# Opening stage of an attention and two-layer-pair kernel: idle and row-sum products left out, lists written anew, a small load behind each weight half

## The chip, the cores and the metric

The kernel runs on one core of a Trainium2 chip. The metric is the device time of one execution in microseconds (us), measured three times; lower is better. The profile shows five engines that run side by side and wait for each other by semaphores: PE (TensorE: matrix products and, as PEld, the loads of their stationary operand), DVE (VectorE), ACT (ScalarE), POOL (GpSimd, here the issuer of loads) and SP (SyncE, the issuer of most loads and stores).

## The reference

```python
# attention: q, k, v (4, 8, 768, 64), 8 memory keys and values a head
for c in range(nc):                       # chunks of 32 queries
    l_start = max(0, c_start - 16); r_end = min(S, c_end + 8)
    k_full = concat([mem_k, k[l_start:r_end]]); v_full = ...
    scores = scale * q_c @ k_full.T
    scores = scores - max(scores); a = exp(scores)
    a = a / (sum(a) + 1e-9)
    out[chunk] = a @ v_full
x = out as (3072, 512)
h = relu(x @ w_in); x = (s * h * h + b) @ w_out               # 512 -> 2048 -> 512
g = x @ w_gate; out = (g * sigmoid(g) * (x @ w_val)) @ w_out2   # 512 -> 1536 -> 512
```

All data are 32-bit floats. The big products are made of three reduced-precision products each (high times high, high times low, low times high), so every weight and every operand is split into two parts first.

## The kernel before

The tokens are cut into 24 groups of 128 queries (g) and eight blocks of 384 tokens (t). Groups 0 to 5 are the opening stage: their keys and queries come in with a few large loads, are turned on PE against the identity and copied out (`stage_batch_keys`, `stage_batch_queries`; steps K and Q). Then, for each group, follow the scores S (32 products of 32x64, `stage_scores`), the row maximum on DVE, the exponential on ACT, the turning A of the probabilities on PE, the products V with the values (`stage_values`), the division by the row sums on DVE (`stage_normalise`), and the turning X of the result (`stage_turn`), which ACT or DVE round to a high part `xhi`, while DVE makes the residue `xlo` (`stage_x`). Every S, and every V, takes both banks of the pool `ps_a`, so an S or V starts only when the one before it was read out by DVE or ACT.

The first pair of layers has 16 weight slots m (W0 to W15), each loaded in two halves of 512 KB (`load_slot`, `load_w1`) and split by a chain of operations, mostly on DVE (`split`: magnitude, two steps of `t_first`, sign, rest, a rounding copy, a residue). U is the up product of one block with one slot (`first_up`, bank `hp`, 12 products), D the down product (`first_down`, banks `acc`). The first U of block 0 needs X0 to X2, the first of block 1 needs X3 to X5.

For groups 0 to 5 the row sums come from PE: `stage_values` multiplies the turned probabilities with a column of ones as well (line 636), and `stage_sums_out` (lines 658 and 660) reads those sums from the bank. Where a group's name stands in `MOVED` as e0, e6 and so on, ACT makes the sums along with the exponential instead (`stage_exp_heads`). `run_idle` runs products of the identity with itself whose result nobody reads.

A planner (`Plan`) simulates all tasks with fixed durations and emits each engine's instructions in the order it finds. `START` is the order of the opening steps on PE, written out by hand; `LOADS` the order of the big loads on SP; `MOVED` says which tasks go to the second engine of two. SP issues in order and a waiting load holds up those behind it. Values come by POOL's own loads, into three buffers in turn.

Of the kernel before, what the change touches and what calls it, by code (L numbers as in the profile page):

```python
# [30 lines left out]
    "K0 Q0 S0 W24 S1 A0 Q1 V0 A1 S2 X0 K1 V1 A2 X1 V2 S5 X2 S3 U S4 U A3 V3 A4 D X3 V4 D X4 A5 U "  # L31
    "V5 U X5 D U D "
# [12 lines left out]
    "BK1 BK0 C BM BQ01 BQ00 W1 W0 K6_0 BQ10 BQ11 W6 W3 W5 W2 W4 W11 W10 W7 W9 W8 W12 W13 W14 W15 "  # L45
# [15 lines left out]
)  # L61


class Plan:
# [12 lines left out]
    def add(self, engine, length, emit, deps=(), get=(), put=(), lag=0.0, take=(), give=()):  # L77
        t = SimpleNamespace(
            n=len(self.tasks), engine=engine, length=length, emit=emit, get=tuple(get), put=list(put),
# [20 lines left out]

    def run(self):
# [12 lines left out]
        started = []  # L114
        while events:
# [15 lines left out]
            for engine, waiting in ready.items():  # L131
                for item in sorted(waiting) if free[engine] else ():
                    t = self.tasks[item[1]]
                    if all(self.room[r] >= t.get.count(r) for r in t.get):
                        for r in t.get:
                            self.room[r] -= 1
                        waiting.remove(item)
                        free[engine] = False
                        t.start = now
                        started.append(t)  # L140
                        heapq.heappush(events, (now + t.length, 0, t.n))
                        break
# [5 lines left out]
def attention_and_two_mlps(  # L148
# [70 lines left out]
    kept = const.tile([P, PAD + P + PAD + 3], F32, name="ident")  # L219
    padded, sb, ones = (kept[:, a:z] for a, z in ((0, 2 * PAD + P), (2 * PAD + P, 2 * PAD + P + 2), (2 * PAD + P + 2, 2 * PAD + P + 3)))  # L220
    ident = padded[:, PAD:PAD + P]
    make_identity(nc, ident)
    nc.vector.memset(ones, 1.0)
# [19 lines left out]
    def load_slot(sources, name, rows="(k p) f -> p k f"):  # L243

        raw = wp.tile([P, 2, 2 * 512], U32, tag="w", name=f"raw_{name}")
        for n, src in enumerate(sources):
# [6 lines left out]
            else:  # L253
                nc.sync.dma_start(out=raw[:, n], in_=src)
        return raw

    raw1 = {}
    w1 = {}

    def load_w1(m):  # L260
        cols = slice(m * P, (m + 1) * P)
        raw1[m] = load_slot((w_in[:, cols], w_out[cols, :]), f"first{m}", "(p k) f -> p k f")
# [231 lines left out]
    def load_memory_values():  # L494
        for e in range(2):
            nc.gpsimd.dma_start(
                out=lent("keys1")[0:NMEM, 3, e * NP * D:(e + 1) * NP * D].rearrange("p (j d) -> p j d", d=D),
# [3 lines left out]
    def load_values(g, queue):  # L501
# [3 lines left out]
        for e in range(2):  # L505
            p0 = e * KC
            if g < VBUFS(0):
                mem = lent("keys1")[0:NMEM, 3, e * NP * D:(e + 1) * NP * D]
# [59 lines left out]
    def stage_max(g, e):  # L568
        gi = g % GB
        ps = staged[g]["s"][e]  # L570
        if e == 0:
            staged[g]["mx"] = ap_.tile([P, 2, NC, 1], F32, tag="mx", name=f"mx{g}")
# [32 lines left out]
    def stage_exp_heads(g, e):  # L605
        if e == 0:
            staged[g]["rc"] = ap_.tile([P, NC, 2, 1], F32, tag="rc", name=f"rc{g}")
# [18 lines left out]
    def stage_values(g, both=None):  # L626
        at = staged[g].pop("at")
        tv = loaded.pop(g)["v"]
        n = D + (g < EARLY)
        banks = [t[:, -NC * n:].rearrange("p (c s) -> p c s", c=NC) for t in both or two_banks(f"psV{g}")]  # L630
# [13 lines left out]
    def stage_sums(g, done=False):  # L644
        if not done:
            staged[g]["rc"] = ap_.tile([P, NC, 2, 1], F32, tag="rc", name=f"rc{g}")
# [8 lines left out]
    def stage_sums_out(g):  # L655
        staged[g]["rc"] = rc = ap_.tile([P, NC, 2, 1], F32, tag="rc", name=f"rc{g}")
        for e in range(2):
            nc.vector.tensor_scalar(rc[:, :, e], staged[g]["o"][e][:, :, D:], 1e-9, None, op0=ALU.add)
        flat = rc.rearrange("p c e o -> p (c e o)")
        nc.vector.reciprocal(flat, flat)  # L660

    def stage_normalise(g, e):
        if e == 0:
            staged[g]["on"] = ap_.tile([P, 4 * 2 * D], F32, tag="on", name=f"on{g}")
        on, o, n = staged[g]["on"], staged[g]["o"][e][:, :, :D], D // KD
# [895 lines left out]
```

## Time and profile before

| | us |
|---|---|
| three runs | 1212.52, 1213.50, 1213.93; median 1213.5 |
| profiled execution | 1214.94 |
| its span in the trace | 1213.1 |
| PE busy / DVE busy | 1185.6 / 744.9 |

The profiled execution is 1.84 us longer than its span, and 1.4 us longer than the median. PE is busy for 98% of the span, so time can only be lost where PE waits, runs products that aren't needed, or runs at the lower clock. The rows show where: nearly all of it lies before 90 us.

### The profile page before, as it was taken

How to read it: one execution, taken by the hardware profiler on the slowest of the kernel's cores; microseconds unless marked ns; L12 is line 12 of the kernel's file. 1: busy time of each engine (PE TensorE's matmuls, PEld its weight loads, DVE VectorE, ACT ScalarE, POOL GpSimd, SP SyncE). 2: the span in 40 equal slices, each digit the busy share in tenths (PEclk: the TensorE clock that was granted, in tenths of full speed). 3: DMA queues.
4: the chain of work that ended last, by engine and by line, in shares of the span. 5: the costliest groups of instructions: out<-in, count | busy, mean ns of one | idle time of the engine just before them, and what ended most of it. 6: DMA issues, size and time to landing. Idle time of an engine off the chain costs nothing.

```text
span 1213.1 us, 24661 instructions
## 1 busy us (share of the span) xinstructions
PE 1185.6 (98%) x9872; PEld 1130.9 (93%) x9872; DVE 744.9 (61%) x1309; ACT 505.1 (42%) x894; POOL 145.9 (12%) x235
## 2 busy tenths in 40 slices
PE   7699999999999999999999999999999999999998
PEld 6589999999999999999999999999999999999997
DVE  5699976655554445444487956569854367743343
ACT  4336543243333443342276545446433235432332
POOL 4750013222222223120000000000000000000000
PEclk9799999999999999999999999999999999999999
DMA  9754334322222222220356256386555386465351
GB/s 281 177 154 145 113 104 98 68 44 65 42 52 66 44 65 51 44 54 1 113 199 236 121 218 229 122 309 255 201 221 217 127 330 247 153 245 208 108 206 52
DMA packets 160991, 175.49 MB, mean 145 GB/s; under 512 B 101276, under 2 KB 130252, under 8 KB 159852
## 3 DMA queue, kind: packets, MB, share of 16 engines
q1 hardware_dynamic: 153580, 162.54, 40.9%
q0 software_dynamic: 7296, 11.37, 3.8%
q8 instruction: 78, 1.28, 0.4%
q14 instruction: 37, 0.30, 0.1%
HBM read 124.85 MB, written 48.76 MB: 143 GB/s over the span
## 4 chain that ended last, share of the span: by engine, by line
PE 91%; DVE 4%; issue 2%; SPq 1%; DMA 1%; ACT 1%; DVEq 0%; ACTq 0%
PE hp L701 7%; PE acc L701 6%; PE acc L702 6%; PE hp L703 6%; PE hp L702 6%; PE acc L703 6%; PE chain_A L702 6%; PE chain_A L703 6%; PE oacc L703 6%; PE oacc L702 6%; PE chain_A L701 5%; PE oacc L701 5%; PE chain_B L701 4%; PE chain_B L703 4%; PE chain_B L702 4%
## 5 line engine op out<-in xcount | busy, mean ns | idle before, releaser
L701 PE MATMUL hp<-xhi,w_first 128*128 128x384 f32 x512 | 174.5, 341 | 0.0
L701 PE MATMUL acc<-ghi,w_first 128*128 128x384 f32 x512 | 173.1, 338 | 0.4 <-DVE ghi L754 0.4
L702 PE MATMUL acc<-glo,w_first 128*128 128x384 f32 x512 | 171.6, 335 | 0.8 <-DVE glo L763 0.4
L702 PE MATMUL hp<-xlo,w_first 128*128 128x384 f32 x512 | 172.0, 336 | 0.0
L703 PE MATMUL hp<-xhi,w_first 128*128 128x384 f32 x512 | 172.0, 336 | 0.0
L703 PE MATMUL acc<-ghi,w_first 128*128 128x384 f32 x512 | 171.3, 334 | 0.0
L516 POOL DMA_DIRECT2D v<-in_v_dram x190 | 121.9, 649 | 297.3 <-PE psB L634 273.0
L871 ACT ACTIVATE kept<-chain_A 128x384 f32<-128x384 f32 x144 | 70.8, 492 | 184.9 <-PE chain_A L703 184.4
L702 PE MATMUL chain_A<-ops,hi_up 128*128 128x384 f32 x384 | 130.1, 339 | 0.0
L703 PE MATMUL chain_A<-ops,lo_up 128*128 128x384 f32 x384 | 129.4, 337 | 0.0
L701 PE MATMUL chain_A<-ops,hi_up 128*128 128x384 f32 x384 | 128.4, 334 | 0.0
L741 DVE SCALAR_TENSOR_TENSOR r<-r,ident 128x384 f32<-128x384 f32 x89 | 54.5, 612 | 114.0 <-ACT r L730 112.4
L730 ACT ACTIVATE r<-hp 128x384 f32<-128x384 f32 x100 | 49.1, 491 | 170.0 <-PE hp L703 158.1
L703 PE MATMUL oacc<-w_down,glo 128*128 128x512 f32 x288 | 114.6, 398 | 0.0
L702 PE MATMUL oacc<-w_down,ghi 128*128 128x512 f32 x288 | 113.9, 396 | 0.0
L701 PE MATMUL oacc<-w_down,ghi 128*128 128x512 f32 x288 | 112.1, 389 | 0.0
L702 PEld LDWEIGHTS acc<-glo,w_first 128*128 128x128 f32 x512 | 96.1, 188 | 2.0 <-DVE glo L763 1.2
L701 PEld LDWEIGHTS hp<-xhi,w_first 128*128 128x128 f32 x512 | 96.7, 189 | 1.4 <-issue 0.2
L701 PEld LDWEIGHTS acc<-ghi,w_first 128*128 128x128 f32 x512 | 96.1, 188 | 1.6 <-DVE ghi L754 0.7
L876 DVE TENSOR_TENSOR kept<-chain_B,kept 128x384 f32<-128x384 f32 x48 | 26.7, 557 | 114.7 <-PE chain_B L703 112.5
L702 PEld LDWEIGHTS hp<-xlo,w_first 128*128 128x128 f32 x512 | 96.7, 189 | 0.2 <-DVE xlo L696 0.2
L703 PEld LDWEIGHTS hp<-xhi,w_first 128*128 128x128 f32 x512 | 96.7, 189 | 0.0
(171 smaller groups left out, 2270.5 us busy)
## 6 DMA issues: line engine op xcount, KB each, us to landing
ops<-ops_dram SPq DMA_DIRECT2D x56, 768.0 KB
ops_dram<-ops SPq DMA_DIRECT2D x28, 768.0 KB
sum_dram<-o SPq DMA_DIRECT2D x48, 256.0 KB
v<-in_v_dram POOLq DMA_DIRECT2D x162, 56.0 KB, 2.9
raw_first<-in_moe_w_in_dram SPq DMA_DIRECT2D x16, 512.0 KB
raw_first<-in_moe_w_out_dram SPq DMA_DIRECT2D x16, 512.0 KB
o<-sum_dram SPq DMA_DIRECT2D x8, 1024.0 KB
y_dram<-y SPq DMA_DIRECT2D x32, 192.0 KB
```

The source lines that it names most:

```text
L516: queue.dma_start(out=tv[p0 + row:p0 + row + rows, c].rearrange("p (j d) -> p j d", d=D), in_=v[b, e:H:2, first:first + rows, :].rearrange ...
L701: nc.tensor.matmul(o, whi, xhi, start=first, stop=False, skip_group_check=onto)
L702: nc.tensor.matmul(o, whi, xlo, start=False, stop=False, skip_group_check=onto)
L703: nc.tensor.matmul(o, wlo, xhi, start=False, stop=last, skip_group_check=onto)
L730: nc.scalar.activation(out=r, in_=hp, func=AF.Relu)
L741: nc.vector.scalar_tensor_tensor(out=r, in0=r, scalar=s_sb, in1=r, op0=ALU.mult, op1=ALU.mult)
L871: nc.scalar.activation(out=t, in_=st2[n]["A"], func=AF.Copy)
L876: nc.vector.tensor_tensor(out=t, in0=st2[n]["B"], in1=kept, op=ALU.add)
```

## The change

- The 24 idle products (step W24) and the products with ones are left out, and with them the ones column. The row sums of groups 0 to 2 now come from ACT with the exponential (e0, e1, e2), those of groups 3 to 5 from a reduction on DVE over the exponentials (`stage_sums`, new line 664).
- `START`, `LOADS` and `MOVED` are written anew. Q1 now stands ahead of A0, S1 and S2 ahead of K1, V0 behind K1, S4 and V3 ahead of the first U. The constants `s`, `b` and the memory keys are loaded behind the first block of keys, ahead of the second; all queries ahead of all weights. More copies go to DVE: three of the first four key banks, two of A, two of `xhi`.
- `load_slot` with `follow` issues behind each half of a W slot a load of one element into one of two cells. Two loads into the same cell wait for each other, so this small load is issued only once the small load two halves back has landed.
- The planner counts PE's instructions (`words`) and holds PE at every 256th until the next 256 have come (`PAGE`, `FETCH`, `end`). Slots, sums and buffers (`rc0` to `rc2`, `vb0` to `vb2`, `s0` to `s3`) are given back by name. The memory values lie in the `values` buffer. This acts on the order alone.

```diff
 START = (
-    "K0 Q0 S0 W24 S1 A0 Q1 V0 A1 S2 X0 K1 V1 A2 X1 V2 S5 X2 S3 U S4 U A3 V3 A4 D X3 V4 D X4 A5 U "
-    "V5 U X5 D U D "
+    "K0 Q0 S0 Q1 A0 S1 S2 K1 V0 A1 S3 X0 V1 A2 X1 V2 A3 S4 X2 V3 U A4 S5 X3 U V4 A5 D X4 U D V5 "
+    "U X5 D U D "
 )
 LOADS = (
-    "BK1 BK0 C BM BQ01 BQ00 W1 W0 K6_0 BQ10 BQ11 W6 W3 W5 W2 W4 W11 W10 W7 W9 W8 W12 W13 W14 W15 "
+    "BK0 C BM BK1 BQ01 BQ00 K6_0 BQ11 BQ10 W1 W0 W2 W3 W7 W4 W5 W12 W6 W8 W10 W9 W14 W11 W13 W15 "
 )
 MOVED = (
-    "a10 a12 a9 e0 e6 g0_0 ...
+    "a0 a10 a12 a4 a7 a9 e0 e1 e2 e6 e8 g0_12 ...
...
+DEPTH = 2
+PAGE, FETCH = 256, ((45.0, 8.3), (110.0, 4.0), (1e9, 2.5))
...
+    probe = const.tile([1, DEPTH], F32, name="probe")
+    probes = [probe[:, n:n + 1] for n in range(DEPTH)]
...
-    def load_slot(sources, name, rows="(k p) f -> p k f"):
+    def load_slot(sources, name, rows="(k p) f -> p k f", follow=False):
...
                 nc.sync.dma_start(out=raw[:, n], in_=src)
+            if follow:
+                probes.append(probes.pop(0))
+                nc.sync.dma_start(out=probes[-1], in_=s_row)
...
-    def run_idle(n):
-        ps = bank(ps_acc, "acc0", "idle")[:, 0:P]
-        for _ in range(n):
-            nc.tensor.matmul(ps, ident, ident, start=True, stop=True)
...
-                nc.tensor.matmul(banks[e][rows_to, col, :D], at[r, col, rows_to], tv[r, c, j], start=True, stop=True)
-                if n > D:
-                    nc.tensor.matmul(banks[e][rows_to, col, D:], at[r, col, rows_to], ones[r], start=True, stop=True)
+                nc.tensor.matmul(banks[e][rows_to, col], at[r, col, rows_to], tv[r, c, j], start=True, stop=True)
```

PE, the first V. Before, it comes behind Q1, each product with one by ones behind it (psQ are banks of turned queries, psK of turned keys, psV of V):

```order
L343 MATMUL psQ_2_476<-ident,queries_277 64x128 x6
L343 MATMUL psQ_3_484<-ident,queries_277 64x128 x6
L634 MATMUL psV_0_495<-v_150,at_461 32x64
L636 MATMUL psV_0_495<-ident,at_461 32x1
L634 MATMUL psV_1_496<-v_150,at_461 32x64
L636 MATMUL psV_1_496<-ident,at_461 32x1
```

Now it comes behind the second turning of the keys, and the rows by ones are gone:

```order
L366 MATMUL psK_0_517<-ident,keys_143 64x69 x12
L366 MATMUL psK_1_539<-ident,keys_143 64x69 x12
L366 MATMUL psK_2_554<-ident,keys_149 64x69 x12
L366 MATMUL psK_3_576<-ident,keys_149 64x69 x12
L651 MATMUL psV_0_609<-v_214,at_453 32x64
L651 MATMUL psV_1_610<-v_214,at_453 32x64
```

What moved: V0 went past S2 and K1, and halved its count of instructions.

SP, the first weight slots. Before, they are issued ahead of the second batch of queries, one half behind the other:

```order
L333 DMA keys_145<-in_mem_k_dram 8x8x64
L327 DMA queries_155<-in_q_dram 128x4x192 x2
L249 DMA raw_first_162<-in_moe_w_in_dram 128x4x256
L254 DMA raw_first_162<-in_moe_w_out_dram 128x1024
L249 DMA raw_first_197<-in_moe_w_in_dram 128x4x256
```

Now all queries go ahead, and each half is followed by the load of one element:

```order
L350 DMA queries_219<-in_q_dram 128x4x192 x2
L268 DMA raw_first_238<-in_moe_w_in_dram 128x4x256
L276 DMA probe<-in_mem_k_dram 1x1
L273 DMA raw_first_238<-in_moe_w_out_dram 128x1024
L268 DMA raw_first_259<-in_moe_w_in_dram 128x4x256
```

What moved: the weights stand behind the queries, and no more than three halves can be under way when a small load is let through.

DVE, the row sums. Before, they are read from the bank of V, ten short rows in all for groups 1 to 5, right ahead of the division (on):

```order
L999 SCALAR_TENSOR_TENSOR raw_first_446<-raw_first_446,t_first_652 128x1024
L658 TENSOR_SCALAR rc_789<-psV_0_701 128x4
L658 TENSOR_SCALAR rc_789<-psV_1_702 128x4
L660 RECIPROCAL rc_789<-rc_789 128x8
L673 TENSOR_TENSOR on_793<-psV_0_701,rc_789 128x4x64
```

Now, for group 3, they are reduced from its exponentials (values is the scratch they lie in), before its V:

```order
L704 TENSOR_TENSOR xlo_728<-psO_719,xhi_727 128x4x128
L1008 SCALAR_TENSOR_TENSOR raw_first_359<-raw_first_359,t_first_537 128x1024
L664 TENSOR_REDUCE rc_788<-values 128x8
L667 TENSOR_SCALAR rc_788<-rc_788 128x8
L668 RECIPROCAL rc_788<-rc_788 128x8
```

What moved: the sum no longer stands between V and the division, but it is a longer instruction.

## Rows read from the trace of the kernel before

**Rows 1.** The page, part 1: busy time, share of the span, instructions.

```profile
PE 1185.6 (98%) x9872; PEld 1130.9 (93%) x9872; DVE 744.9 (61%) x1309; ACT 505.1 (42%) x894; POOL 145.9 (12%) x235
```

**Rows 2.** Stretches: length; PE, PEld, DVE, ACT, POOL busy; clock; DMA share; GB/s.

```profile
30.00:40.00 10.00, 4.66 (x122) 3.81 (x124) 4.69 (x9) 3.00 (x6) 6.84 (x11) 0.73 1.10 261
40.00:50.00 10.00, 6.87 (x212) 6.58 (x209) 5.21 (x8) 5.20 (x7) 5.80 (x9) 0.58 0.85 174
...
120.00:150.00 30.00, 29.79 (x231) 29.03 (x230) 29.29 (x44) 18.85 (x44) 0.00 (x0) 1.00 0.39 113
```

**Rows 3.** PE in order of time: start, length, instructions, idle time before and releaser.

```profile
7.66 0.98 PE L276 MATMUL spread<-ident,sb_in 1*128 1x1 f32 x4 [7.66 <-DMA sb_in<-in_moe_s_dram]
...
9.01 5.57 PE L343 MATMUL psK<-ident,keys 128*64 128x69 f32 x96
...
19.18 4.96 PE L380 MATMUL idle<-ident 128*128 128x128 f32 x42 [0.18 <-issue]
...
26.89 1.97 PE L343 MATMUL psQ<-ident,queries 128*64 128x128 f32 x32 [0.36 <-issue]
...
35.34 0.21 PE L636 MATMUL psV<-ident,at 64*32 64x1 f32 x1 [5.35 <-issue]
...
43.55 4.63 PE L343 MATMUL psK<-ident,keys 128*64 128x69 f32 x75 [2.91 <-issue]
...
49.18 0.16 PE L636 MATMUL psV<-ident,at 64*32 64x1 f32 x1 [0.21 <-issue]
```

**Rows 4.** The same view: products of the first U, second U, block 1, slot 14.

```profile
62.05 0.52 PE L702 MATMUL hp<-xlo,w_first 128*128 128x384 f32 x1
...
66.36 0.33 PE L701 MATMUL hp<-xhi,w_first 128*128 128x384 f32 x1
...
88.93 0.34 PE L701 MATMUL hp<-xhi,w_first 128*128 128x384 f32 x1
...
167.85 0.33 PE L701 MATMUL hp<-xhi,w_first 128*128 128x384 f32 x1
```

**Rows 5.** DVE's waits from 13 to 89 us: total, times, longest.

```profile
DVE rc L658 <- PE psV L636: 5.5, 2, 5.0
DVE on L673 <- PE psV L636: 5.2, 1, 5.2
...
DVE mx L576 <- PE psS L565: 1.7, 1, 1.7
DVE qt L240 <- PE psQ L343: 0.9, 1, 0.9
```

**Rows 6.** DVE in order of time: first key copy, residue of X5, residue of slot 14.

```profile
13.46 0.86 DVE L240 COPY early_klo<-psK 128x672 f32<-128x672 f32 x1 [4.16 <-PE psK L343]
...
88.37 0.68 DVE L696 TENSOR_TENSOR xlo<-psO,xhi 128x512 fp32r<-128x512 f32 x1
...
155.74 1.23 DVE L1048 TENSOR_TENSOR w_first<-raw_first,w_first 128x1024 fp32r<-128x1024 f32 x1
```

**Rows 7.** DVE's instructions by line: count, busy us, mean ns, idle before.

```profile
L999 DVE SCALAR_TENSOR_TENSOR raw_first<-raw_first,t_first 128x1024 uint32<-128x1024 uint32 x7 | 8.6, 1224 | 0.2
...
L990 DVE TENSOR_SCALAR t_first<-t_first 128x1024 f32<-128x1024 f32 x7 | 4.9, 706 | 0.0
...
L696 DVE TENSOR_TENSOR xlo<-psO,xhi 128x512 fp32r<-128x512 f32 x6 | 4.1, 682 | 0.0
L592 DVE TENSOR_TENSOR queries<-psS,mx 128x256 f32<-128x256 f32 x6 | 2.2, 416 | 0.0
...
L658 DVE TENSOR_SCALAR rc<-psV 128x4 f32<-128x4 f32 x10 | 1.2, 160 | 5.6 <-PE psV L636 5.5
```

**Rows 8.** DVE's row-sum reduction of later groups: ns min/median/max.

```profile
L649 DVE TENSOR_REDUCE rc<-sc x17: 641/648/687, 173.0 to 559.0; 128x8 f32<-128x512 f32 x17
```

**Rows 9.** The page, part 3, the queue of instructions: packets, MB, share.

```profile
q8 instruction: 78, 1.28, 0.4%
```

**Rows 10.** POOL in order of time: its first wait for a load.

```profile
5.39 0.18 POOL L523 COPY v<-keys 1x1 f32<-1x1 f32 x1 [4.08 <-DMA keys<-in_k_dram]
```

More of the change, by code (lines that the diff above doesn't have):

```diff
@@ L99, in after, with end @@
         return d.lag + (0.0 if d.engine == t.engine else 0.25)
+    def end(self, t, now):
+        left, rest = t.words, t.length
+        while left:
+            n = min(left, PAGE - self.word % PAGE)
+            now, rest, left = now + rest * n / left, rest - rest * n / left, left - n
+            self.word += n
+            if self.word % PAGE == 0:
+                now = max(now, self.next)
+                self.next = now + (next(us for at, us in FETCH if now < at) if self.word > PAGE else 4.0)
+        return now
     def run(self):
@@ L114, in run @@
         started = []
+        self.word, self.page, self.next = 0, 0.0, 0.0
         while events:
@@ L140, in run @@
                         started.append(t)
-                        heapq.heappush(events, (now + t.length, 0, t.n))
+                        heapq.heappush(events, (self.end(t, now) if engine == "PE" else now + t.length, 0, t.n))
                         break
@@ L628, in stage_values @@
         tv = loaded.pop(g)["v"]
-        n = D + (g < EARLY)
-        banks = [t[:, -NC * n:].rearrange("p (c s) -> p c s", c=NC) for t in both or two_banks(f"psV{g}")]
+        banks = [t[:, -NC * D:].rearrange("p (c s) -> p c s", c=NC) for t in both or two_banks(f"psV{g}")]
         for c, j, rows_to, col in places(g):
@@ L962, in load_v @@
             v_ = transfer(
-                [batch_landed["VM"]] if first else [], lambda: load_values(g, nc.sync), n, 460, take=["v"],
+                [batch_landed["VM"]] if first else [], lambda: load_values(g, nc.sync), n, 460, take=[f"vb{g % VBUFS(g)}"],
                 rate=208.0, name=f"V{g}",
@@ L967, in load_v @@
             issue = plan.add(
-                "POOL", 0.65 * n, lambda: load_values(g, nc.gpsimd), [batch_landed["VM"]] if first else [], take=["v"]
+                "POOL", 9.2 if first else 0.65 * n, lambda: load_values(g, nc.gpsimd), [batch_landed["VM"]] if first else [],
+                take=[f"vb{g % VBUFS(g)}"],
             )
-            v_ = plan.add(MOVE, 2.4, None, [issue], lag=2.0)
+            v_ = plan.add(MOVE, 1.8 if first else 2.4, None, [issue], lag=5.0 if first else 2.5)
         for e in range(2 if g >= EARLY and g % GB < VBUFS(g) else 0):
@@ L1128, in plan_batch_keys @@
                 f"m{u}_{i}", {ACT: 0.40, DVE: 0.30}, lambda e, i=i: fill_batch_memory(e, u, i),
-                [batch_landed["m"], *(done[:1] if not u else early_ready["q", 1, "pe"])],
+                [batch_landed["m"], *(done[:1] if not u else early_ready["q", 0, "pe"] + early_ready["q", 1, "pe"])],
             ))
@@ L1147, in plan_scores @@
     def plan_scores(g, t=None):
-        own = ["own"] if g >= EARLY else ["sc"]
+        own = ["own"] if g >= EARLY else [f"s{g % len(SCRATCH)}"]
         give = ["a"] if t is None else []
@@ L1152, in plan_scores @@
                 u = g // GPB
-                ready, back = (*early_ready["k", u], *early_ready["q", u]), ["x"] + ["r"] * NP if g == GPB - 1 else []
+                ready, back = (*early_ready["k", u], *early_ready["q", u]), []
+                scored.setdefault(u, [])
             else:
@@ L1156, in plan_scores @@
             t = plan.add(
-                PE, 1.00, lambda: stage_scores(g), ready, take=["a", "a"], give=back, lag=0.2 if g < EARLY else 0.0
-            )
+                PE, 1.00, lambda: stage_scores(g), ready, take=["a", "a"], give=back, lag=0.2 if g < EARLY else 0.0,
+                words=128,
+            )
+            if g < EARLY:
+                scored[u].append(t)
+                if len(scored[0]) == GPB and not u:
+                    plan.add("NONE", 0.0, None, scored[0], give=["x"] + ["r"] * NP)
         t = plan.add(DVE, 0.34, lambda: stage_max(g, 0), [t])
@@ L1164, in plan_scores @@
                 t = plan.add(
-                    ACT, 1.0, lambda e=e: stage_exp_heads(g, e), [t], give=give, take=[*own, "rc"] if e == 0 else ()
+                    ACT, 1.0, lambda e=e: stage_exp_heads(g, e), [t], give=give, take=[*own, f"rc{g % 3}"] if e == 0 else ()
                 )
@@ L1172, in plan_scores @@
         at_[g]["n"] = plan.add(ACT, 0.54, lambda: stage_exp(g), [t])
-        at_[g]["rc"] = None if g < EARLY else plan.add(
-            DVE, 0.90, lambda: stage_sums(g), [at_[g]["n"]], take=["rc"]
+        at_[g]["rc"] = plan.add(
+            DVE, 0.90, lambda: stage_sums(g), [at_[g]["n"]], take=[f"rc{g % 3}"]
         )
@@ L1280, in plan_down1 @@
                 PE, 2.08 / KD, lambda i=i: first_down(t, m, i),
-                [g_ready[t, m], *(acc_free[i:i + 1] if begins(t, m) else ())],
+                [g_ready[t, m], *(acc_free[i:i + 1] if begins(t, m) else ())], words=6,
                 put=["w"] if last and t == NB - 1 else (), give=["ghi", "glo"] if last else (),
@@ L1383, in plan_y @@
         plan.add(
-            DVE, 0.01, None, [y_ops[key, op] for op in range(1, 8)], give=["yq"],
+            "NONE", 0.0, None, [y_ops[key, op] for op in range(1, 8)], give=["yq"],
             put=["w"] * 3 + ["wt"] * (s == NS - 1),
@@ L1464, in attention_and_two_mlps @@
             plan_batch_keys(g)
-        elif what == "W":
-            plan.add(PE, 0.16 * g, lambda g=g: run_idle(g), take=["acc0"])
-            plan.rings["acc0"].append(plan.last_pe)
         elif what == "S":
```

80 lines of the change are left out of this document (44 added, 36 removed), and 24 rows, old and new, of the table MOVED.

## The prediction

> **What bounds the kernel now.** First the busy times: PE works 98% of the span [rows 1], so the question is what can be taken out of PE's 27.5 us of idle time, of its needless products and of its slow stretches. Then the busy times by stretch: between 30 and 50 us PE is busy 11.5 of 20 us, the granted clock averages 0.73 and 0.58, and the DMA engines are full (share 1.10 and 0.85) [rows 2]. From 89 us on PE hardly waits. So the change is worth what it moves the first U of block 1, which starts at 88.93 [rows 4]: what follows is PE at its own pace, 1213.1 - 88.9 = 1124.2 us, and the change leaves its products alone.
>
> Next PE in order of time up to there. Its first product waits 7.66 us for the constants. Then it stops at 19.18, 26.89, 35.34, 43.55 and 49.18, each time for nothing that the profile shows ("issue") [rows 3]. Between the stops at 35.34 and 43.55 it ran 127 products, each with a load of its operand, 254 instructions; the queue of instructions moved 1.28 MB in 78 packets, 16.4 KB each [rows 9]. I read the stops as PE out of code: a block of some 256 instructions comes every 7.7, 8.5, 8.2 and 5.6 us, and PE uses it up faster. The 48 idle products (96 instructions) and the 64 products by ones in each V (128 instructions, 384 up to V2) use up code that the work behind them waits for.
>
> Last DVE, since PE's stops hand their time on. From its first key copy at 13.46 to the residue of X5, which ends at 88.97 and lets the first U of block 1 go [rows 6], DVE waits 5.5 + 5.2 + 1.7 + 0.9 = 13.3 us [rows 5], and works the other 62.2 of 75.5. Its two long waits (5.0 and 5.2) are for V0 and V1, behind the stops at 35.34 and 43.55. So in this stage DVE is the fuller engine: with PE never out of code it would still have 62 us of work to do after the first keys. The path that I sum is DVE's: start, plus work, plus waits.
>
> **The change part by part.**
>
> *Start.* The constants now queue behind one block of keys (0.79 MB), not two. The first of two blocks had landed by 5.39, when POOL's wait for it ended [rows 10], the constants behind both at 7.66. I take PE's start at 5.7, near the first row. PE needs 9.01 - 7.66 = 1.35 us to the first key product and 5.57 / 4 = 1.4 us a bank [rows 3]; DVE takes the first bank itself now, at 5.7 + 1.35 + 1.4 + 0.2 = 8.7 instead of 13.46. Gain 4.8; bounds 3 (start at 7.5) and 5.
>
> *DVE's work up to X5*, counted in the order of both kernels up to that residue. Added: three copies of key banks at 0.86 [rows 6], 2.6; four copies of 128x512 (two A, two `xhi`) at 0.68, by the residue of that size [rows 7], 2.7; two fills with memory keys, a quarter of a bank copy, 0.5; three reductions at 0.65 [rows 8], 1.95; of splitting one more sign step at 1.22 and one more short step at 0.71, less one rounding copy of about that price [rows 7], 1.2; seven short rows at 0.16, 1.1. Taken away: four subtractions at 0.42 (1.7), ten short rows of sums at 0.16 (1.6) [rows 7], and of U's tiles two squares and a relu, about 0.55 each by the rows on either side in size (1.7). Net 2.6 + 2.7 + 0.5 + 1.95 + 1.2 + 1.1 - 5.0 = 5.1 us more work; bounds 4 and 7. This is the price of the change: DVE and ACT do what PE did in code that came too late.
>
> *DVE's waits.* Four are built into the new order. While PE turns the keys DVE is ahead of it: 1.4 us a bank against 0.86 and a fill, about 2.0 up to the fourth bank. Then S0, whose 64 products must end behind the last query bank, an estimate of 2.0. Then Q1: before it PE needs the second block of code; 180 instructions are used when K0 is almost done, at 11.7, and the next block takes 5.4 (what the one at 19.18 took from the same place, near 13.8) to 8.5 us, so Q1 starts between 17.1 and 20.2, and with A0 behind it DVE waits 0 to 3, I take 1.4. The next blocks run out in S2 (long there by then), in K1's last quarter and in S3's last third. In K1 the stop costs DVE nothing, since it has W0 and W1 to split (two slots, ten steps of 0.7 to 1.2) while V0 waits. In S3 it may: 0 (5.6 us a block, [rows 3] at 49.18) to 5 (8.5 a block, and no split ready), taken as 1.0. Later stops fall into V2 and V3, where DVE has the splits of W2 to W4; V2's data, a queue of POOL's loads that now starts 2 us later because it waits for the second block of keys, adds 0 to 2; 0.9 together. Sum 2.0 + 2.0 + 1.4 + 1.0 + 0.9 = 7.3, against 13.3 before; bounds 4 and 16.
>
> *Idle products.* They stood where PE waited for both banks of S0, so as time they were free, as code they weren't; that is in the stops. The granted clock is the other thing that they may have held up. It averaged 0.73 from 30 to 40 us, with PE idle for half of it [rows 2], in spite of them, and the first U ran at the lower of the two levels (1.2 of 2.4 GHz): 0.52 us a product against 0.33 in the second [rows 4], at most 12 x 0.19 = 2.3 us for its twelve. The Trainium skill, TensorE: Matmul & The Clock Gate, Part 1, says that the lower clock is the default and that activity releases it, which speaks against taking idle products out. Should U0 and U1 both run low now, PE needs up to 2.3 us more than before; DVE, busy with splits, hides it or lets at most that through.
>
> *The small loads.* Each costs SP an issue and a wait; behind it queue the next weight half and the quadrant loads of group 6, which DVE turns only after X5. Keys, queries and five slots are 3.1 + 5.2 = 8.4 MB, at 261 GB/s [rows 2] 32 us; W1 and W0, the first two, are in by some 20, and DVE comes to W0 near 23. Nobody waits; 0, bounds -2 (code comes sooner) and +2. The Trainium skill, DMA: Bandwidth & Descriptors, Queues, rings and completion order, says that each DMA engine takes the queues that have work in turn, packet by packet. By it code, on a queue of its own, would wait no less behind a short queue of weights than behind a long one, and the small loads would buy nothing: S3's stop at its upper end, 1211.8 in place of 1207.8. The stops agree that code is slow while the engines are full (8.2 us) and quicker at half load (5.6) [rows 2, 3]; no row tells a short full queue from a long one.
>
> *Sum.* 4.8 (start) - 5.1 (work) + 13.3 - 7.3 (waits) = 5.7 us earlier at the first U of block 1. Behind it DVE has about as much to split in either kernel and is nearly full (29.3 of 30 us from 120 to 150 [rows 2]); the residue of slot 14 ended at 157.0, its first U at 167.85 [rows 4, 6], so PE can come 6 us sooner without meeting it. The profiled execution should take 1214.9 - 5.7 = 1209.2 and the median, which is 1.4 us under it, 1213.5 - 5.7 = 1207.8.
>
> **The rivals.**
>
> *Only the built-in waits stay.* If small loads and shorter code keep PE supplied, DVE waits the 4.0 of keys and S0 and little else: 4.8 - 5.1 + 13.3 - 4.0 = 9.0, 1204.5. For it: up to the first U PE needs 344 instructions fewer behind Q0, 1.3 blocks, and does V3 besides. Against it: the chain S, exponential, next S through two banks leaves gaps.
>
> *The small loads don't do what they say*, because code waits for full engines and not for a long queue (the rule above), or because SP's issues, each of which waits for the load eight back, held back the weights already: S3's stop 5 instead of 1. Gain 1.7, 1211.8, hardly told from no change.
>
> *Slower.* The stops hit DVE as before: K1's and S3's arrive when no slot is ready to split, so that the 12.4 us of DVE's waits other than for queries recur on top of the new 4.0. 4.8 - 5.1 + 13.3 - 16.4 = -3.4: 1216.9. It decides from waits of 13.0 on. For it: the DMA engines have the same 8.4 MB to bring. Against it: three slots are in before V0.
>
> *A weight or value comes late*, V2's data behind POOL's later start above all: 2 to 3 us, 1210 to 1211, inside the forecast's edge.
>
> **How the numbers follow.** Forecast (1205.5 to 1210.5) 0.50; only the built-in waits (1200 to 1205.5) 0.20; small loads or late data (1210.5 to 1214) 0.18; slower (above 1214) 0.12. What a measurement of this kernel can tell from no change is 0.2%, 2.4 us: 1211.1 to 1215.9. Faster than that 0.75, within it 0.15, slower 0.10. Below 1199 or above 1214 I leave 0.16. The range 1199 to 1214 takes in both ends of the start, the work and the clock, and waits from 4 to 13.
>
> **What would show it.** PE's first product near 5.7; DVE's first copy near 8.7; waits of DVE from there to the residue of X5 near 7; the first U of block 1 near 83; no "issue" stop above 3 us; V's products in half the instructions; no split later than its U between 100 and 170. It is wrong if PE's stops keep their 5 us, if U of block 1 starts at the same time while DVE never waits (then its added work was mis-sized), or if PE, ahead by 6 us, begins to wait for slots after 100 us.

## The result, and the profile after

The changed kernel takes 1221.52 us (median of 5 runs, 1218.97 to 1222.62) against 1213.5 for the kernel before: ratio 1.0061, 95% interval 1.0045 to 1.0077. It is slower by 8 us, where 5.7 us less were forecast. Its profiled execution spans 1220.7 us, against 1213.1.

PE's busy time falls (first line of the page's part 1: busy us and share, instructions), against [rows 1], but it is idle for longer:

```profile
PE 1179.4 (97%) x9440; PEld 1122.6 (92%) x9440; DVE 750.7 (61%) x1315; ACT 508.1 (42%) x924; POOL 146.3 (12%) x235
```

The stretches from 20 to 60 us hold most of that (columns as in [rows 2]; the granted clock is the third number from the end). From 30 to 60 us PE now works 11.6 of 30 us; from 40 to 60 it runs at the lower of its two levels throughout (0.50):

```profile
20.00:30.00 10.00, 5.44 (x178) 4.71 (x180) 9.68 (x20) 6.33 (x26) 7.75 (x12) 0.66 1.07 269
30.00:40.00 10.00, 3.65 (x126) 2.93 (x121) 7.72 (x11) 7.68 (x23) 7.71 (x13) 1.00 0.92 166
40.00:50.00 10.00, 4.98 (x136) 3.67 (x136) 4.22 (x9) 1.70 (x3) 8.05 (x13) 0.50 0.93 230
50.00:60.00 10.00, 2.97 (x71) 2.41 (x72) 8.84 (x14) 3.94 (x6) 3.37 (x6) 0.50 0.74 119
```

PE in order of time answers to [rows 3, 4]:

```profile
5.87 0.98 PE L299 MATMUL spread<-ident,sb_in 1*128 1x1 f32 x4 [5.87 <-DMA sb_in<-in_moe_s_dram]
...
33.09 0.70 PE L366 MATMUL psK<-ident,keys 128*64 128x69 f32 x16 [1.87 <-issue]
...
44.14 1.39 PE L651 MATMUL psV<-v,at 64*32 64x64 f32 x64 [1.40 <-issue]
...
55.66 1.13 PE L688 MATMUL psO<-ident,on 128*128 128x128 f32 x4 [9.09 <-DVE on L681]
...
92.45 0.66 PE L709 MATMUL hp<-xhi,w_first 128*128 128x384 f32 x1 [4.52 <-DVE xhi L256]
```

The start is as forecast (5.87 for 5.7), and so is the supply of code: in place of stops of 5.35 and 2.91 us there are 1.87 and 1.40. But PE stands 9.09 us in front of X1 and 4.52 us in front of the first U of block 1, for DVE each time. That U starts at 92.45; before it was 88.93 [rows 4], the forecast was 83. ACT and DVE show what DVE waited for:

```profile
48.63 1.12 ACT L993 ACTIVATE t_first<-raw_first 128x1024 f32<-128x1024 f32 x1 [8.30 <-DMA raw_first<-in_moe_w_out_dram]
49.65 0.59 ACT L254 ACTIVATE xhi<-psO 128x512 fp32r<-128x512 f32 x1
...
55.40 1.18 ACT L993 ACTIVATE t_first<-raw_first 128x1024 f32<-128x1024 f32 x1 [4.65 <-DMA raw_first<-in_moe_w_out_dram]
...
87.87 1.12 ACT L993 ACTIVATE t_first<-raw_first 128x1024 f32<-128x1024 f32 x1 [8.87 <-DMA raw_first<-in_moe_w_out_dram]
```

```profile
89.02 0.69 DVE L999 TENSOR_SCALAR t_first<-t_first 128x1024 f32<-128x1024 f32 x1 [3.98 <-ACT t_first L993]
...
91.61 0.69 DVE L256 CAST xhi<-psO 128x512 fp32r<-128x512 f32 x1
```

ACT's magnitude steps (L993) of W4, W5 and W6 stand for slots that have not landed. ACT takes its instructions in order, and behind the step for W4 stands the copy that X0's residue needs (49.65, `xhi`), behind that everything up to X1. At 87.87 it is W6: DVE has W6's next step (L999) queued ahead of X5's cast (91.61), and X5 is what the U at 92.45 waits for. W4 is multiplied only after 110 us: nobody needed that step yet. In all ACT stands 24.3 us at such slots, and SP 18.2 us at small loads:

```profile
ACT t_first L993 <- DMA raw_first<-in_moe_w_out_dram: 24.3, 4, 8.9
```

```profile
SPq L276 <- DMA probe<-in_mem_k_dram: 18.2, 12, 2.7
```

The books: 3.5 us late at that U; 2.7 more behind it, since PE, after its wait, runs the U itself at the lower level (the granted clock is 0.66 from 90 to 100); 1.3 between 600 and 700 us, where PE works 98.37 of 100 us and worked 99.64 before. Together 7.5 of the 7.6 us between the two spans.

### The profile page after: what moved, and what is told of

It is laid out like the page before. It is cut to its first block, busy times and chain, and to the rows that moved or that the text cites. A ratio compares the mean times of both kernels' runs of the same rounds, so it can differ in the third digit from the quotient of the medians.

```text
span 1220.7 us, 23848 instructions
## 1 busy us (share of the span) xinstructions
PE 1179.4 (97%) x9440; PEld 1122.6 (92%) x9440; DVE 750.7 (61%) x1315; ACT 508.1 (42%) x924; POOL 146.3 (12%) x235
## 4 chain that ended last, share of the span: by engine, by line
PE 89%; DMA 4%; DVE 4%; SPq 1%; issue 1%; ACT 0%; DVEq 0%; ACTq 0%
PE hp L709 7%; PE acc L709 7%; PE acc L710 7%; PE acc L711 7%; PE hp L710 7%; PE hp L711 7%; PE chain_A L710 5%; PE oacc L711 5%; PE oacc L710 5%; PE chain_A L711 5%; PE chain_A L709 5%; PE oacc L709 5%; PE chain_B L709 4%; PE chain_B L711 4%; PE chain_B L710 4%; DMA probe<-in_mem_k_dram 2%
## 5 line engine op out<-in xcount | busy, mean ns | idle before, releaser
L738 ACT ACTIVATE r<-hp 128x384 f32<-128x384 f32 x94 | 46.1, 490 | 162.2 <-PE hp L711 151.1
```

What stands on the lines that cost most here:

```text
L738: nc.scalar.activation(out=r, in_=hp, func=AF.Relu)
```

## The experiments

Times are medians; each ratio is to runs of the kernel before on the same chip (1213.3 to 1214.5). Runs of different pairs were on different chips, so between them the ratios tell more than the medians. "U1" is the start of the first U of block 1 in the profiled execution.

**Small loads.** Theory 1 was that they make slots late; the rival, theory 2, that the new lists do. Three runs: the changed kernel without them, the kernel before with them alone (the same lines added to its `load_slot`), and the changed kernel with four in flight.

```
-        raw1[m] = load_slot(..., "(p k) f -> p k f", True)
+        raw1[m] = load_slot(..., "(p k) f -> p k f")
```

> The changed kernel without its small loads: SP issues each half of a weight slot right behind the last; lists, idle products and products with ones stay as changed. Theory 1 (the small loads keep SP from issuing, so the slots of W4, W5 and W6 land late, and ACT and DVE, which take their instructions in order, stand at these slots' magnitude steps): SP's waits on them in the changed kernel were 18.2 us in 12, so SP comes to W4 some 10 to 15 us sooner, W4 lands near 40 instead of 48.6, ACT's waits for slots fall from 24.3 us to under 8, X1 no longer waits 9.09 us, and the first U of block 1 starts 4 to 9 us sooner than 92.45: 1212 to 1217. Theory 2 (the new list of loads, five slots and then 16 loads of key and query quadrants ahead of W4, makes it late by itself): W4 still lands after 46, ACT waits over 18 us, and the time stays within 1219 to 1223. If code then comes late again (theory 3: the small loads do what they are for), PE stops over 3 us for nothing that the profile shows come back between 17 and 45 us.

> The kernel before with the small loads alone: each half of a first-product weight slot is followed by one, two in flight. Theory 1 (small loads make slots late): the six slots that were issued by 25.6 us are issued near 33, W4 after 42, and ACT or DVE stand for slots; 1216 to 1224. Theory 2 (they cost nothing, the lists do): 1211 to 1216. Theory 3 (they bring code sooner, as they are meant to): PE's stops of 5.35 and 2.91 us at 35.34 and 43.55 shrink below 2, and the time falls to 1206 to 1211.

> The changed kernel with four small loads in flight instead of two: each waits for the one four halves back. Theory 1 (SP's wait is the cost): SP's waits on small loads halve, from 18.2 us to 6 to 12, W4 lands 3 to 8 us sooner, and the time lies between the changed kernel and the one without small loads, 1214 to 1220. Theory 2 (the list of loads): no change, 1219 to 1223.

Measured: 1218.56 (1.0044, 1.0031 to 1.0056); 1213.27 (0.9996, 0.9986 to 1.0006); 1220.78 (1.0055, 1.0039 to 1.0070). So small loads cost the changed kernel 2 to 3 us (the intervals overlap) and the kernel before nothing; with four in flight SP waits for slot halves to land instead (8.0 and 5.8 us are the largest sums). Without them SP still issues W4 behind 14 quadrant loads, at 39.63 in place of 40.54, and ACT waits 7.70 for it in place of 8.30. Theory 1 explains a third of the loss at most. In the kernel before they do a part of what they are for: its stop of 5.35 us in V0 becomes 2.50, though the next two are 2.78 and 1.91 in place of 2.91 and 0.21, and all stops up to 131 us sum to 8.6 in place of 10.9. Its sixth slot is issued at 34 us in place of 21, and ACT begins to wait for slots. The time stays level:

```profile
ACT t_first L991 <- DMA raw_first<-in_moe_w_out_dram: 10.8, 3, 6.0
...
PE psV L643 <- issue: 4.6, 3, 2.5
```

**Idle products.** The kernel before without them, and the changed kernel with them back behind S1, at no length in its planner, so that every other instruction keeps its place.

```
-    "K0 Q0 S0 W24 S1 A0 Q1 ...
+    "K0 Q0 S0 S1 A0 Q1 ...
```

> The kernel before without its 24 idle products (48 instructions of PE, which compute nothing); all else stays. If they were only code that the work behind them waits for, PE's stops of 5.35 and 2.91 us at 35.34 and 43.55 come 48 instructions later in the work or shrink by one fifth of a block's time (1 to 2 us), and the time falls by 0 to 2 us: 1211.5 to 1213.5. If they hold the granted clock up, more of the first U tiles run at the lower level: the first two U run at 0.52 us a product, DVE hides part of it, and the time rises by 0 to 3 us: 1213.5 to 1216.5.

> The changed kernel with its 24 calls of idle products put back, behind S1, where PE stands 2.85 and 0.77 us for the exponentials of S0 and S1; every other instruction keeps its place on every engine. Theory 3 (the idle products hold the granted clock, and taking them out of the kernel before cost 3.8 us by itself): the granted clock from 20 to 30 us is 1.0 instead of 0.66, fewer products run at the lower level up to the first U, the first U of block 1 starts 2 to 5 us sooner than 92.45, and the time is 1215 to 1219. Theory 2 (the late slots decide, the clock in that stretch is covered by the waits): within 1.5 us of the changed kernel, 1220 to 1223; the stop in K1 grows, since 96 instructions more come ahead of it.

Measured: 1217.62 (1.0030, 1.0013 to 1.0046) and 1223.43 (1.0074, 1.0055 to 1.0093). In the kernel before they are worth 3.8 us (1.6 to 5.6 by the interval), more than either range that was expected. Without them its runs spread from 1214.3 to 1222.2 us, and the profiled one, 1221.22, is among the longest; the rows below are of that one. In it the clock is 0.66 from 20 to 30 us, and the stops for code don't shrink: the 5.35 of V0 becomes 1.11 in V0 and 4.88 in S2:

```profile
20.00:30.00 10.00, 6.25 (x130) 5.25 (x131) 9.79 (x18) 6.60 (x22) 7.29 (x11) 0.66 1.07 264
```

```profile
37.86 0.54 PE L565 MATMUL psS<-early_khi,qt 64*32 64x64 f32 x19 [4.88 <-issue]
```

In the changed kernel they bring the clock of that stretch back to 1.00 and nothing else: it falls to 0.66 in the next, and X1 still waits 8.89 us. Of three further pairs, below, one is 1.8 us faster with them and two are 1.2 and 2.9 us slower. How much of the 3.8 us is clock and how much is where the stops fall isn't settled.

**Products with ones**, replaced in the kernel before by DVE's reduction, with three buffers for the sums in place of one. The planner moves steps of ACT, DVE and SP with it:

```
-                if n > D:
-                    nc.tensor.matmul(banks[e][rows_to, col, D:], at[...], ones[r], ...)
...
+        at_[g]["rc"] = plan.add(DVE, 0.90, lambda: stage_sums(g), ...)
```

> The kernel before with the row sums of groups 1 to 5 by a reduction of DVE (0.65 us each) in place of the products with ones; idle products and lists stay. If those products cost PE code that comes late, its stops of 5.35 and 2.91 us in V0 and V1 go or move behind the V, the first U of block 1 starts 2 to 5 us sooner, and the time is 1208.5 to 1212. If DVE's work is what counts in this stretch, its five reductions, 3.3 us, less the ten short rows of sums, 1.6, leave it 1 to 2 us slower: 1214 to 1216. Two stops at other places in the work would leave it at 1212 to 1215.

Measured: 1214.41, ratio 1.0000 (0.9990 to 1.0010). U1 starts at 82.22, 6.7 us sooner than before, and the time does not change. Behind it PE waits for the split of the next U's result:

```profile
95.28 0.45 PE L699 MATMUL acc<-ghi,w_first 128*128 128x384 f32 x1 [2.29 <-ACT ghi L238]
96.56 0.53 PE L700 MATMUL acc<-glo,w_first 128*128 128x384 f32 x1 [0.83 <-DVE glo L759]
```

By the first scores of group 6 (129.73, before 130.77) one microsecond is left of the 6.7. Of the 5.7 that go, 3.2 are PE's waits; the rest are products at the lower level behind them (the granted clock is 0.96 over the stretch, 1.00 before). That is a finding of its own: up to some 130 us DVE has no slack to give (from U1 to there it works 45.29 of 47.51 us, and worked 39.66 of 41.84 before), and PE, ahead of it, waits for it and for ACT.

**W4 and W5 ahead of the quadrants** on SP, without small loads; then with idle products.

```
-    "... W1 W0 W2 W3 W7 W4 W5 W12 W6 ..."
+    "... W1 W0 W2 W3 W7 W4 W5 K6_1 W12 W6 ..."
```

> The changed kernel without small loads, and with W4 and W5 ahead of the key and query quadrants of group 6 in SP's queue (five slots, W4, W5, then the quadrants), where the changed kernel has 14 quadrant loads ahead of W4. Theory 2 (the list of loads makes W4 and W5 late): SP issues W4 when the keys' room is given back, near 36, instead of 39.6; W4 lands near 42 and W5 near 46 instead of 47.3 and 53.8, ACT's long wait of 7.70 us for W4 falls below 3, X1 does not wait 8.1 us, and the time falls by 3 to 6 us under that without small loads, 1212.5 to 1215.5. If the room in the pool or the DMA engines themselves hold W4, it lands after 46 and the time stays within 1217 to 1220.

> The same as the run with W4 and W5 ahead of the quadrants, without small loads, and with the 24 calls of idle products back behind S1. If late slots and the missing idle products each cost what they seem to, both gains add: 1208 to 1213, level with the kernel before or ahead of it. If they cover one another (PE waits in the stretch either way), it is within 1.5 us of the run without idle products.

Measured: 1220.72 (1.0054, 1.0039 to 1.0070) and 1218.90 (1.0038, 1.0027 to 1.0049). A miss for the time, a hit for the mechanism: X1 starts 1.7 us sooner than without the change of order, and its wait falls from 8.10 to 5.36 us. But SP comes to W12 and W6 only at 70 and 72 us, W6 lands near 83 (the DMA engines have a share of 0.91 from 70 to 80), ACT stands 8.4 us at W6, DVE 5.4 behind ACT, and X5 waits for DVE:

```profile
86.33 1.13 PE L688 MATMUL psO<-ident,on 128*128 128x128 f32 x4 [6.34 <-DVE on L681]
```

**The planner told how late the slots land**: its landing times of W4 to W6, W8 to W10, W12 and W14 moved by 8 to 18 us. PE's order stays; with small loads, without, and without but with idle products.

```
+LATE = {4: 8, 5: 12, 12: 15, 6: 18, 8: 18, 10: 15, 9: 8, 14: 8}
-        return plan.add(MOVE, kilobytes / rate, ..., lag=1.8, give=give)
+        return plan.add(MOVE, kilobytes / rate, ..., lag=1.8 + late, give=give)
```

> The changed kernel, small loads and all, with one thing told to its planner: that W4, W5, W6, W8, W9, W10, W12 and W14 land 8 to 18 us later than it thinks, as they do in the trace. PE's and POOL's orders stay word for word; ACT's magnitude steps of W4 to W6 move behind the copies of X0 and X1, which they stood ahead of, and DVE's steps follow. Theory 1 in its narrower form (it is not the late landing that costs, since W4 is not multiplied before 100 us, but that ACT and DVE stand at it in order while X0's copy is queued behind): ACT's waits for slots fall from 24.3 us to under 10, the waits of PE of 9.09 us at X1 and 4.52 us at the first U of block 1 go, and the time falls by 4 to 8 us, 1213.5 to 1217.5. Theory 4 (DVE is full up to there whatever the order, so what it doesn't wait for early it has to do late): the waits go, but the first U of block 1 still starts after 90, and the time stays within 1219 to 1223.

> The same late landings told to the planner, and no small loads. Theory 1: the gain of each adds, 3 us and 4 to 8 us: 1210 to 1214.5. Theory 4: as without small loads alone, 1217 to 1220.

> The same late landings told to the planner, no small loads, and the 24 calls of idle products back behind S1. If the idle products hold the clock, it is 1.0 from 20 to 30 us and the time is 1 to 3 us under that of the run without them; if the clock falls further on anyway, where PE waits (it averaged 0.50 from 40 to 60 us), no change or up to 1 us more, for the code that they use.

Measured: 1234.23 (1.0174, 1.0153 to 1.0194), 1229.91 (1.0135, 1.0116 to 1.0154), 1231.06 (1.0141, 1.0118 to 1.0164). The largest miss, and the most telling. U1 starts at 81.20, 11 us sooner than in the changed kernel, with next to no wait; so it was the order of ACT and DVE in front of late slots that held it, and DVE is not too full to be there by 81. Then all is lost again:

```profile
81.20 0.41 PE L710 MATMUL hp<-xhi,w_first 128*128 128x384 f32 x1 [0.25 <-DVE xhi L257]
...
102.86 0.69 PE L710 MATMUL acc<-ghi,w_first 128*128 128x384 f32 x1 [10.52 <-DVE ghi L257]
```

```profile
100.63 0.49 ACT L739 ACTIVATE r<-hp 128x384 f32<-128x384 f32 x1 [13.00 <-DMA part_dram<-y]
```

ACT's relu waits for a buffer that holds block 0's partial sums, and their stores stand on SP behind slots.

**Old lists, new code**: the changed code with the three lists of the kernel before, idle products among them, without small loads.

> The changed code (no products with ones, its planner with blocks of code and finer room) with the three lists of the kernel before, its idle products among them, and without small loads. PE's order is word for word that of the kernel before without ones (1214.4), the others follow the planner. Theory 2 (the new lists are what costs): 1211 to 1216, level with the kernel before. Theory 5 (the new planner's durations, not the lists, put ACT's and DVE's steps where they wait): 1217 to 1222.

Measured: 1222.22 (1.0071, 1.0052 to 1.0091). PE's order is that of the run without ones (1214.4), so the 7.8 us between them (by the ratios 8.6) are the new planner's places for ACT's, DVE's, SP's and POOL's instructions. Theory 2 falls in its first form: the lists alone are not it. PE waits here at S5 for a step of DVE that stands behind a split step and a wait for a slot, and again idles from 600 to 700 us (98.12 of 100):

```profile
55.23 1.49 PE L588 MATMUL psS<-queries,turned 64*32 64x64 f32 x64 [5.74 <-DVE on L686]
```

```profile
54.15 0.69 DVE L1000 TENSOR_SCALAR t_first<-raw_first 128x1024 uint32<-128x1024 uint32 x1 [2.33 <-DMA raw_first<-in_moe_w_out_dram]
54.76 0.75 DVE L686 TENSOR_TENSOR on<-psV,rc 128x256 f32<-128x256 f32 x2
```

**Stores of the partial sums on POOL's queue**, with the late landings; first with all of them, then with W4 to W6 alone, each with and without small loads.

```
-        nc.sync.dma_start(out=(y_dram[t] if m == M1 - 1 else part_dram[t])[:, i, :], in_=...)
+        queue, to = (nc.sync, y_dram) if m == M1 - 1 else (nc.gpsimd, part_dram)
+        queue.dma_start(out=to[t][:, i, :], in_=...)
```

> The changed kernel with small loads, with the late landings told to the planner, and with the eight stores of block 0's and block 1's partial sums issued by POOL, which has nothing to do from 90 to 130 us, in place of SP, where they stood behind slots. If the order of ACT and SP is what costs, ACT's wait of 13.0 us for a store goes below 3, PE's wait of 10.52 us at the first D of block 1 below 2, the first U of block 1 stays near 81, and the time falls by 8 to 12 us under the 1234.2 without this, 1222 to 1226, less what else PE waits for up to 170 us (2.4 us). If late slots come back behind it (slots not split when their U is due), PE waits over 3 us for splits between 100 and 400 us and the time stays above 1226.

> The same without small loads. If the order is what costs: the first U of block 1 near 80, no wait of PE above 2 us up to 130, and 8 us less than the 1229.9 without stores on POOL in so far as nothing else waits there: 1215 to 1222. If the slots themselves are late: over 1225.

> The changed kernel with small loads, with only W4, W5 and W6 told late (8, 12 and 18 us), the other slots left as the changed kernel thinks, and the stores on POOL. If the three slots at which ACT and DVE stood are the loss: first U of block 1 near 81, no long wait behind it, 1209 to 1215. If the slots behind them are late as well: PE waits for splits after 100 us, and the time is 1216 to 1226.

> The same without small loads: 2 to 4 us under the run with them, 1206 to 1212, if slots come sooner where they are waited for; no change if they aren't waited for any more.

Measured: 1236.38 (1.0193, 1.0175 to 1.0212), 1233.89 (1.0167, 1.0151 to 1.0183), 1230.78 (1.0141, 1.0125 to 1.0157), 1225.89 (1.0094, 1.0076 to 1.0112). ACT's wait for a store falls from 13.0 to 4 or 5 us, U1 stays at 80 to 82, and the time does not fall: now DVE stands at loads that have not landed, with U1 done. In the last of them DVE first waits 7.02 us for ACT, which still stands 5.08 us at a store, and then 5.35 us for a slot, W9:

```profile
93.05 0.49 ACT L739 ACTIVATE r<-hp 128x384 f32<-128x384 f32 x1 [5.08 <-DMA part_dram<-y]
```

```profile
94.86 0.36 DVE L257 CAST ghi<-r 128x384 fp32r<-128x384 f32 x1 [7.02 <-ACT r L748]
...
101.17 0.69 DVE L997 TENSOR_SCALAR t_first<-raw_first 128x1024 uint32<-128x1024 uint32 x1 [5.35 <-DMA raw_first<-in_moe_w_out_dram]
```

SP comes to W9 only at 94.39, behind four other slots. From 54 to 80 us it issues quadrant loads of groups 6 and 7 one behind the other, some 0.47 us apart where it doesn't wait (4.2 us for loads to land), one slot among them (W12, 66.51), the next (W6) only at 80.41:

```profile
55.44 0.43 SPq L464 DMA_DIRECT2D qt<-in_q_dram  x1
55.91 0.43 SPq L460 DMA_DIRECT2D kin<-in_k_dram  x1
...
66.51 0.56 SPq L269 DMA_DIRECT2D raw_first<-in_moe_w_in_dram  x1
67.11 0.62 SPq L274 DMA_DIRECT2D raw_first<-in_moe_w_out_dram  x1
...
80.41 0.56 SPq L269 DMA_DIRECT2D raw_first<-in_moe_w_in_dram  x1
```

From 60 to 70 us the DMA engines have a share of 0.52: what is scarce there is SP's turn, not bandwidth. Hence the last pair.

**Slots first on SP**, against the run above, without and with idle products. The planner's landing times are made to match, so ACT's and DVE's orders change with SP's; PE's and POOL's stay.

```
-    "... W1 W0 W2 W3 W7 W4 W5 W12 W6 W8 W10 ..."
+    "... W1 W0 W2 W3 W4 W5 W6 W7 K6_11 W12 W8 K7_0 W10 ..."
```

> The run without small loads, with known landings and with stores on POOL, and its list of loads in another order: the first eight slots in the order in which they are multiplied (W4 fifth in place of W7), W5, W6 and W7 ahead of most quadrants of group 6, W12 and W8 ahead of all of group 7. PE's order is that of the changed kernel. If the order on SP's queue is what makes slots late: eight slots are issued by 50 and ten by 75 us (in the run before: seven by 43, eight at 67, nine at 81), DVE's waits for slots fall below 2 us up to 110, the first U of block 1 starts near 81, PE's waits behind it up to 130 stay below 3 us together, and the time falls to 1206 to 1213, ahead of the kernel before or level with it. If it is the DMA engines (full until 35 us, half full from 50 on) or the room in the pool, DVE still stands at a slot for over 5 us and the time stays above 1218.

> The same with the 24 calls of idle products back behind S1, all orders otherwise word for word. If the idle products are worth something once slots no longer decide: the clock from 20 to 30 us 1.0 in place of 0.67, and 1 to 4 us less than without them. If the stretch is covered by DVE, which is full there, no change; 1 us more if the code that they use is then missing in K1.

Measured: 1211.78 (0.9991, 0.9981 to 1.0000) and 1214.70 (1.0006, 0.9998 to 1.0015). The first takes 14.1 us less than the run above it and 9.7 less than the changed kernel (by the ratios 12.5 and 8.5). That is the order of loads on SP's queue together with the orders of ACT and DVE that follow from it, and against the changed kernel also the small loads left out and the stores on POOL; what SP's order is worth by itself no run shows. The rows are of an execution of 1214.95 us, the longest of 12, whose span (1213.2) is that of the kernel before. Eight slots are issued by 56 us (hoped for by 50), ten by 70.24; up to 130 us DVE waits for none and ACT 5.2 us for two, behind which DVE waits 1.5 us at most, and U1 starts where this change should have put it. It is level with the kernel before, at the edge of ahead; with idle products it is 2.9 us slower, in spite of a clock of 1.00 in place of 0.66 from 20 to 30 us.

```profile
81.43 0.41 PE L710 MATMUL hp<-xhi,w_first 128*128 128x384 f32 x1 [0.32 <-DVE xhi L257]
...
94.11 0.44 PE L710 MATMUL acc<-ghi,w_first 128*128 128x384 f32 x1 [1.54 <-DVE ghi L257]
```

```profile
80.00:90.00 10.00, 9.46 (x54) 8.92 (x53) 9.89 (x14) 8.38 (x12) 4.71 (x9) 1.00 0.77 190
90.00:100.00 10.00, 8.31 (x37) 7.73 (x36) 9.24 (x14) 6.55 (x10) 0.27 (x1) 0.83 0.57 150
```

From U1 to the first scores of group 6 it takes 46.4 us (127.84 - 81.43), where the kernel before takes 41.8 (130.77 - 88.93): of 7.5 us that PE is ahead, it gives back 4.6, some 2 of it in waits for a DVE that works 9.89 and 9.24 of 10 us, the rest in products at the lower level behind them (the clock is 0.83 from 90 to 100). Another 2.1 go from 600 to 700 us, where PE works 97.55 of 100 us.

## Why the prediction was wrong

*The start*: right. PE at 5.87 for 5.7, DVE's first copy at 8.92 for 8.7.

*Code*: right. No stop above 3 us; the stops of 5.35, 2.91 and 0.21 us became 1.87 and 1.40, with V in half the instructions. In the kernel before, taking the products with ones out moves U1 by 6.7 us, though not by shorter code alone: PE has less to do, and other engines' steps move.

*DVE's added work*: right. From its first key copy to the end of X5's residue DVE is busy for 65.95 us, and was for 60.88: 5.1 more, as in the sum. The stretch in the kernel before, in the changed kernel, and in the run with slots first (columns as in [rows 2]):

```profile
13.46:89.06 75.60, 60.72 (x1549) 55.17 (x1545) 60.88 (x115) 32.65 (x61) 49.36 (x77) 0.86 0.78 193
```

```profile
8.92:93.03 84.11, 54.18 (x1165) 46.80 (x1161) 65.95 (x118) 38.98 (x95) 52.96 (x82) 0.79 0.83 198
```

```profile
8.86:82.01 73.15, 54.03 (x1165) 46.56 (x1161) 65.87 (x118) 39.34 (x95) 52.98 (x81) 0.84 0.93 227
```

*DVE's waits*, 7.3 with bounds 4 and 16, and *the small loads* with their "Nobody waits; 0, bounds -2 and +2": this is the step that failed. DVE is idle for 84.11 - 65.95 = 18.2 us, over the upper bound. Ten of them are the 6.0 us at X0's copy and the 3.98 at W6's step, both waits of ACT first, for slots that had not landed; "nobody waits" looked at W1 and W0 and at no slot behind them. With slots in time DVE is idle for 73.15 - 65.87 = 7.3 us, as forecast, and U1 starts 7.5 us sooner than before, for 5.7 in the sum. The small loads themselves cost 2 to 3 us. The larger part is what else stands on SP's queue: the order of loads was read for who is first, not for what stands ahead of W4, W12 and W6. Ahead of W12 and W6 it is mostly issues of 0.47 us. Ahead of W4 it is that and full DMA engines: in the run without small loads its 14 quadrant loads take from 21 to 39.6 us, 11.7 of them waits of SP for earlier loads to land.

The rival "a weight comes late" had the mechanism and priced it at 2 to 3 us, a single lateness; it missed that the waiting instruction stands in order ahead of the path's own steps, and that the slots behind are late by as much. The rival "slower" had the direction, at 0.12, by stops of PE that did not come. The prediction priced the small loads by what queues behind them on SP, and did not ask the same of ACT's steps for slots.

Three readings of the kernel before were off as well. DVE's idle time up to X5's residue is 75.60 - 60.88 = 14.7 us there, for 13.3: the rest is gaps too short for [rows 5]. And the residue is not what let the first U of block 1 go: its row in [rows 4] has no idle time, PE was busy up to it. And the block of code that came within 5.6 us did not come "at half load": from 40 to 50 us the DMA share is 0.85 [rows 2].

*The clock*: 2.3 us at most, hidden, was too little in one place. The first U of block 1 ran at the lower level behind its wait of 4.5 us, 2.7 us on the path. That idle products are free as time fits the changed kernel and its variants (four pairs, from 1.8 us faster with them to 2.9 slower) and was wrong for the kernel before (3.8 us).

*Behind U1*: "PE can come 6 us sooner without meeting it" was wrong too, hidden by the first error. It compared slot 14's residue with its U, and no slot in between. Without ones 5.7 of 6.7 us are lost by 130 us, with slots first 4.6 of 7.5. So the forecast of 1207.8 would not have come out with slots in time either: that run takes 1211.8. And the 1.3 to 2.1 us from 600 to 700 us, a stretch in which I had PE "at its own pace", belong to the new planner, since the run with old lists has them too.

Not settled: which of the new planner's durations puts split steps ahead of the steps that PE waits for, what the order on SP's queue is worth with ACT's and DVE's orders held, and what of the idle products' 3.8 us is clock.

## What to carry to other kernels

When loads share one queue, count for each load that someone waits for how many issues stand ahead of it, at the price of one issue in the trace: a queue of small loads is late even where the DMA engines are half idle. In an engine that works in order, a step for data that may be late belongs behind the steps of the path, even if it seems to fill a gap; a wait there costs what is queued behind it. And before a start some microseconds sooner is counted as a gain, look for the first engine that is full behind it: here two kernels brought PE forward by 7 us and kept 1 to 3.

## What the runs showed of the hardware

SP's quadrant loads of 16 KB cost some 0.47 us of SP each, one behind the other, with the DMA engines at a share of 0.52 from 60 to 70 us: the 45 of them between 54 and 80 us are 21 us without a slot, but for one. An issue can take longer in itself while many loads ahead of it are out: without small loads the second halves of the fourth and fifth slot took 3.38 and 3.53 us to issue, for 0.62 just before (the line's start and length); with small loads, and so with few halves out, the same two took 0.35. That a full queue is what holds the issue is a reading, which no row shows:

```profile
12.14 0.62 SPq L273 DMA_DIRECT2D raw_first<-in_moe_w_out_dram  x1
...
13.40 3.38 SPq L273 DMA_DIRECT2D raw_first<-in_moe_w_out_dram  x1
...
17.41 3.53 SPq L273 DMA_DIRECT2D raw_first<-in_moe_w_out_dram  x1
```

Whether code comes sooner behind a short queue of loads stays open. For it: the kernel before with small loads stops for 8.6 us in place of 10.9, and the changed kernel's stops up to 50 us are 3.3 us together with them and 6.1 without (1.68, 3.07 and 1.39). Against it: the run with slots first, which has no small loads, stops for 3.6. The Trainium skill, DMA: Bandwidth & Descriptors, Queues, rings and completion order, says that a DMA engine goes round the queues that have work, packet by packet; from that it would follow that the length of the other queue does not matter to code. These rows do not decide it, since the stops also fall at other places of the work.
